# Order of ScalarE's casts at an expert's start, and a new order of all steps, in an attention and mixture-of-experts kernel

## The chip, the cores and the metric

The kernel runs on one core of a Trainium2 chip. The metric is the device time of one execution in microseconds; the median of several runs counts. TensorE (PE; PEld is its weight load) multiplies, VectorE (DVE) and ScalarE (ACT) work element by element, GpSimd (POOL) does some of that and issues the indirect DMAs, and SyncE (SP) issues all other DMAs from one queue.

## The reference

Two parts. Attention over q, k, v of shape 2 x 8 x 576 x 64: the sum of a pooled attention (q, k, v averaged over groups of 4 positions, 144 x 144 scores, the result repeated 4 times) and a local one (positions less than 4 apart). Then a mixture of 8 experts on the 1152 rows of 512:

```python
x = out.transpose(0, 2, 1, 3).reshape(B * S, H * D)        # 1152 x 512
logits = x @ w_gate                                        # 8 experts
e = argmax(logits); g = softmax(logits)[e]                 # one expert a row, up to capacity 288
y = maximum(x_e @ w1[e], 0) @ w2[e]                        # 512 -> 1024 -> 512
out[row] = g * y
```

## The kernel before

The rows are cut into ten tiles L0 to L9 (each two blocks of 58 positions), the pooled attention into eight parts P0 to P7. Routing goes in groups of tiles (K0: tiles 0 and 1, K1: 2 to 5, K3: 6 and 7, K4: 8 and 9). The experts are ranked by their number of rows and run one after the other, expert 0 first, with 192, 184, 160, 160, 152, 120, 112 and 88 row slots.

All five engines run an order that is written out by hand, in two lists of steps, `PLAN` (attention and routing, to the start of the first expert) and `PLAN2` (experts). `run` and `run2` take one step after the other and emit its instructions; each engine executes its own in this order and waits for data by semaphore. So the lists are the queues. The steps that matter here:

- `Lt.sc, mx, sb, ex, tu, ct, v0, v1, a, r, n`: scores (PE), largest and shift (DVE), exp (ACT), transpose (PE), its copy (ACT), values (PE) and their division (DVE) of tile t. `Lt.sp` spreads pooled rows by DMA, `Lt.ad` adds them (POOL; for tile 9 VectorE in two halves, `L9.ad0`, `L9.ad1`, L558), `Lt.xw` stores the rows to DRAM (SP, L584), `ga, cx, lq, lc, lg` are the gate's logits, `hi, lw` split the rows in two parts (ACT, DVE L581).
- `Pj.s, m, g, w, t, c, va, na, nr, nm`: the same for the pooled attention. `S...` and `V...` pool q, k and v, `D...` load (`Ds00` the gate's weights, `Ds10` the capacity `cap_i`, which `C` reads).
- `Kj.e0` to `e4`, `rk`, `pl`: best expert (DVE, L642 on) and rank of each row. `B.` and `R.` rank the experts. `K4.x, K4.y` give the slots' rows (PE L741, DVE L747).
- `Z`, `ZS`: one warm matmul on zeros (L176), to keep TensorE busy; ten more run at the start.
- `G`: gather of an expert's rows (POOL). `T0cp, T0c6` to `T0c9`: expert 0's rows transposed and selected into `pX` (PE, L887 to L896), where c is one of two halves; `T00h, T01h`: their cast to fp32r on ScalarE (L900), `T00l, T01l`: the remainder on VectorE (L902).
- `F`n: load of chunk n, 1 MB of weights (SP, L310); four chunks an expert, two of `w1` and two of `w2`, into five buffers. `Wia`: cast of half a chunk to fp32r (ACT, L327), `Wid`: its remainder in bf16 (DVE, some on POOL, L337). Chunk n is W2n and W2n+1: chunk 0 is W0, W1, chunk 1 W2, W3 (both expert 0's `w1`), chunk 2 W4, W5 and chunk 3 W6, W7 (its `w2`).
- `Uefp, h, f, r, l`: quarter f of expert e's first product (PE, L837 fp32r "hi", L840 bf16 "lo"), its copy, sum, Relu, remainder; its PSUM tile comes from three buffers. `D...` the second product, `Ee.p, y, s` the way out (the scatter is POOL, L989).

A fp32 product is made of three: hi x hi and hi x the remainder of the rows in one fp32r matmul of 2n columns, and the weights' remainder times the rows in bf16. A product that is not in `HI_FIRST` does the lo part first; it needs only `T..h`, the hi part also `T..l`.

```python
nc.scalar.copy(hi, r)                                              # L327, Wia
eng.tensor_tensor(lo, r, hi.bitcast(F32), op=ALU.subtract)         # L337, Wid
nc.scalar.copy(hi, self.pX[c2][:, :, 0:n])                         # L900, T0ch
```

Of the kernel before, what the change touches and what calls it, by code (L numbers as in the profile page):

```python
# [1284 lines left out]
```

## Time and profile before

| what | value |
|---|---|
| median of 3 runs | 217.24 us (216.4 to 217.84) |
| the profiled execution | 218.41 us, span 216.6 us |
| TensorE busy | 202.4 us (93%) |
| VectorE busy | 176.9 us (82%) |
| ScalarE busy | 141.1 us (65%) |
| POOL busy | 94.6 us (44%) |
| DMA | 53.55 MB, mean 247 GB/s |

The span runs from the first to the last instruction on an engine. Shares are means over stages with different limits: the attention to about 88 us, where chains run from engine to engine, and the experts after it. The chain of waits follows the end of the span back to what released each step. A number in brackets behind an instruction is the time that its engine sat idle before it, and what ended that.

### The profile page before, as it was taken

What the parts mean: (1) busy time and instruction counts of PE and PEld (TensorE: products, weight loads), DVE (VectorE), ACT (ScalarE), POOL (GpSimd) and SP (SyncE); (2) the same over time, 40 slices, a digit from 0 to 9 for tenths busy, and PEclk for the clock granted to TensorE, in tenths of its full rate; (3) what the DMA queues carried; (4) which work ended last, traced back from release to release, by engine and by line L of the source; (5) the groups of instructions that cost most, each with busy time, mean ns of one, the idle gap of its engine ahead of it and who ended that gap; (6) DMA issues with size and microseconds to landing.
All of it is one profiled execution on the core that took longest, in us unless ns stands there. A gap on an engine that the chain in (4) does not pass through costs nothing.

```text
span 216.6 us, 5906 instructions
## 1 busy us (share of the span) xinstructions
PE 202.4 (93%) x2270; PEld 175.8 (81%) x2270; DVE 176.9 (82%) x415; ACT 141.1 (65%) x289; POOL 94.6 (44%) x116
## 2 busy tenths in 40 slices
PE   8887999999979999699999999999899999999990
PEld 2565878788867779599999999999799998788880
DVE  1896879777898898589999999977999986799920
ACT  2125474567458552668668899679878989869520
POOL 6705962286241754363319238043380380533041
PEclk9999999999999999889999999999999999999997
DMA  5999977866697749958697978999989999846011
GB/s 122 360 263 211 267 255 124 252 140 179 106 343 213 192 155 289 422 183 280 228 319 297 342 295 266 310 359 357 287 335 348 346 340 326 295 135 254 2 58 34
DMA packets 16011, 53.55 MB, mean 247 GB/s; under 512 B 2059, under 2 KB 7179, under 8 KB 11880
## 3 DMA queue, kind: packets, MB, share of 16 engines
q1 hardware_dynamic: 14312, 48.51, 70.0%
q0 software_dynamic: 1664, 4.60, 6.2%
q8 instruction: 19, 0.31, 0.5%
q14 instruction: 16, 0.13, 0.2%
HBM read 45.84 MB, written 5.01 MB: 235 GB/s over the span
## 4 chain that ended last, share of the span: by engine, by line
PE 50%; DVE 21%; DMA 10%; ACT 8%; issue 6%; POOL 1%; SPq 1%; POOLq 0%; DVEq 0%; ACTq 0%
PE pH L837 10%; DVE wlo L337 8%; DMA wraw<-in_w 7%; PE pY L837 7%; PE pZ L954 5%; PE pH L840 5%; PE pY L840 3%; PE psO L518 3%; ACT whi L327 3%; PE psS L484 3%; DMA QT<-in_qT 2%; PE psG L392 2%; PE psOg L431 2%; PE psT L505 2%; PE psTg L417 2%
## 5 line engine op out<-in xcount | busy, mean ns | idle before, releaser
L337 DVE TENSOR_TENSOR wlo<-wraw,whi 128x1024 bf16<-128x1024 f32 x57 | 71.2, 1274 | 1.5 <-ACT whi L327 1.3
L327 ACT CAST whi<-wraw 128x1024 fp32r<-128x1024 f32 x64 | 64.7, 1049 | 8.1 <-DMA wraw<-in_w 7.1
L837 PE MATMUL pH<-xs,whi 128*128 128x320 f32 (+6 forms) x256 | 42.9, 313 | 0.8 <-DVE yT L971 0.7
L837 PEld LDWEIGHTS pH<-xs,whi 128*128 128x128 f32 x256 | 37.4, 193 | 1.7 <-PE pH L837 0.9
L840 PEld LDWEIGHTS <-wlo 128*128 128x128 bf16 x416 | 29.1, 97 | 6.0 <-issue 2.5
L337 POOL TENSOR_TENSOR wlo<-wraw,whi 128x1024 bf16<-128x1024 f32 x7 | 19.1, 2722 | 33.6 <-ACT whi L327 31.5
L837 PE MATMUL pY<-hs,whi 128*128 128x320 f32 (+3 forms) x160 | 29.3, 326 | 0.0
L989 POOL DMA_INDIRECT out<-y,si x13 | 16.0, 1231 | 30.4 <-ACT y L984 10.6
L868 POOL DMA_INDIRECT XG<-x_dram,gi x13 | 18.0, 1387 | 15.7 <-PE pX L891 11.1
L837 PEld LDWEIGHTS pY<-hs,whi 128*128 128x128 f32 x160 | 24.6, 188 | 0.0
L840 PE MATMUL pH<-xs,wlo 128*128 128x160 bf16 (+6 forms) x256 | 22.2, 231 | 1.8 <-ACT xs L900 1.8
L923 DVE TENSOR_TENSOR hf<-pH,hl 128x320 f32<-128x320 f32 (+6 forms) x32 | 14.3, 453 | 6.0 <-ACT hl L920 5.8
L176 PE MATMUL psW<-idle 128*128 128x512 bf16 x50 | 17.5, 429 | 1.3 <-DVE idle L171 1.0
L920 ACT COPY hl<-pH 128x320 f32<-128x320 f32 (+6 forms) x32 | 12.4, 401 | 9.2 <-PE pH L840 4.7
L925 ACT ACTIVATE hs<-hf 128x320 fp32r<-128x320 f32 (+6 forms) x32 | 13.9, 448 | 6.5 <-DVE hf L923 3.5
L558 POOL TENSOR_TENSOR x<-x,UP 128x512 f32<-128x512 f32 x9 | 11.4, 1276 | 14.8 <-DMA UP<-od 6.1
L927 DVE SCALAR_TENSOR_TENSOR hs<-hf,hs 128x320 fp32r<-128x320 f32 (+6 forms) x32 | 14.5, 471 | 2.1 <-ACT hs L925 2.0
L500 ACT ACTIVATE pt<-pt 128x512 f32<-128x512 f32 x10 | 6.3, 632 | 15.1 <-DVE pt L496 15.1
L374 POOL TENSOR_TENSOR wraw<-wraw 72x512 f32<-72x512 f32 x8 | 10.3, 1286 | 11.0 <-DMA wraw<-in_vp 11.0
L840 PE MATMUL pY<-hs,wlo 128*128 128x160 bf16 (+3 forms) x160 | 14.8, 238 | 0.0
L518 PE MATMUL psO<-VW,pT 64*64 64x65 f32 x320 | 12.3, 221 | 0.9 <-ACT pT L509 0.7
L518 PEld LDWEIGHTS psO<-VW,pT 64*64 64x64 f32 x320 | 10.5, 134 | 3.1 <-ACT pT L509 1.1
(223 smaller groups left out, 358.2 us busy)
## 6 DMA issues: line engine op xcount, KB each, us to landing
wraw<-in_w SPq DMA_DIRECT2D x32, 1024.0 KB, 7.1
x_dram<-x SPq DMA_DIRECT2D x10, 256.0 KB, 2.1
wraw<-in_vp SPq DMA_DIRECT2D x4, 576.0 KB
UP<-od SPq DMA_DIRECT2D x16, 120.0 KB, 3.4
VW<-in_vw SPq DMA_DIRECT2D x2, 780.0 KB
VW<-in_vw SPq DMA_DIRECT2D x2, 520.0 KB
QT<-in_qT SPq DMA_DIRECT2D x2, 476.0 KB
KT<-in_kT SPq DMA_DIRECT2D x2, 476.0 KB, 7.3
```

The costliest lines, as they stand in the source:

```text
L176: nc.tensor.matmul(psW, idle, idle.unsqueeze(1).to_broadcast([128, 4, 128]), start=True, stop=True)
L327: nc.scalar.copy(hi, r)
L337: eng.tensor_tensor(lo, r, hi.bitcast(F32), op=ALU.subtract)
L518: nc.tensor.matmul(psO[64 * blk:64 * blk + 64, k * (D + 1):(k + 1) * (D + 1)], self.pT[64 * blk:64 * blk + 64, hp, 64 * par:64 * par + 64] ...
L837: nc.tensor.matmul(ps[:, 0:2 * n], hi, xs[:, 0:2 * n], start=first and a, stop=last and not a, skip_group_check=True)
L840: nc.tensor.matmul(ps[:, 0:n], lo, upper_half(xs[:, 0:n]), start=first and a, stop=last and not a, skip_group_check=True)
L868: nc.gpsimd.indirect_dma_start(out=xg[0:self.ps[j], :], out_offset=None, in_=x_dram[0:rows, :], in_offset=bass.IndirectOffsetOnAxis(ap=sel ...
L920: nc.scalar.copy(hl[:, :, 0:n], self.pH[f2][:, :, n:2 * n])
L923: nc.vector.tensor_tensor(hf[:, :, 0:n], self.pH[f2][:, :, 0:n], self.hl[f2][:, :, 0:n], op=ALU.add)
L925: nc.scalar.activation(hi, hf[:, :, 0:n], AF.Relu)
L927: nc.vector.scalar_tensor_tensor(self.hs[:, f, n:2 * n], hf[:, :, 0:n], 0.0, hi.bitcast(F32), op0=ALU.max, op1=ALU.subtract)
L989: d = nc.gpsimd.indirect_dma_start(out=out[:, :], out_offset=bass.IndirectOffsetOnAxis(ap=self.token(j), axis=0), in_=self.y[j][0:p, :], i ...
```

## The change

The two lists hold the same steps in another order. Two lines of code move with it, because the exponentials of a group may now come in another order: the sum tile `rz1` is made at whichever comes first. The beginning and the end of `PLAN` and the first lines of `PLAN2` are shown, with the part of `PLAN` that concerns tiles 6 to 9; the rest of the lists is reordered in the same way. `HI_FIRST` stays.

```diff
 PLAN = """
-ZS S00q0 L0.sc ZS ZS ZS L0.mx ZS L0.sb L0.ex Dq01 Dv00 ZS Z L1.sc S00q1 L0.tu S00k0 Dp00 V000 S00k1 L1.mx L1.sb
-L1.ex L3.sc S01k0 Z S01k1 L3.mx L3.sb V001 L2.sc L1.tu L1.ct L1.v0 L2.mx L2.sb Z Ds00 L2.ex P0.s0 P0.m0 P0.m1
...
-P2.nr Dp11 P2.nm L0.cx P5.s0 L1.ad L4.a0 L4.r0 L4.n0 P5.m0 P5.m1 P5.g0 P5.w0 P3.va L1.ga V110 P5.w1 L0.lq Ds10
...
-P7.c0 L6.a1 L6.r0 P6.t1 P6.c1 L8.sc Bg C L4.ad L6.n0 P7.t1 L7.mx L8.mx L8.sb P7.c1 L6.r1 L8.ex L2.lg L6.n1 L3.lg
-K0.s1 L4.ga L4.cx L6.sp K0.s0 Bl L5.ad L5.ga P6.va P6.na L5.cx L4.xw L7.sb L6.ad P6.nr P6.nm P7.va P7.na P7.nr
-L7.ex L5.lq K0.tz K0.ts P7.nm L4.lq ZS L5.lc L7.tu L4.lc L6.hi L4.lg L5.lg L7.ct F0 K1.e0 K1.e1 K1.e2 L8.tu
-K1.z0 L7.v0 L7.v1 K1.e3 ZS L6.lw ZS K1.e4 L7.a0 K1.rk W0a W1a L6.ga ZS L7.r0 ZS F1 K1.z3 L8.ct ZS L7.a1 L7.sp
...
-K1.s3 L8.ad W2a L7.ga L9.sp K1.sl K1.to Ia W0d L9.v0 L9.v1 L9.a0 L8.ga ZS L7.cx L9.a1 ZS L7.hi L7.lw L7.lq ZS
-L6.lg L8.hi L7.lc ZS L9.r0 L9.r1 L9.n0 L9.n1 Z L6.xw L7.lg L9.ad0 K3.e0 K3.e1 K3.e2 L8.cx L9.ad1 G01 L8.lg L8.xw
-K3.e3 K3.e4 L9.ga0 ZS L8.lw K3.z0 L9.ga1 L9.xw F2 K3.z1 L9.hi L7.xw K3.rk ZS ZS L9.cx0 G00 K3.h0 K3.p0 F3 K3.q0
-ZS L9.lw L9.cx1 K3.pl L9.lg0 L9.lg1 T00p K3.tz K4.e0 K4.e1 K4.z0 K4.z1 K4.e2 K4.e3 K4.e4 Rk K4.rk K4.h0 W3a
-K4.pl K4.p0 W4a T01p K3.tn K4.tz W5a Rb Ra T016 K4.q1 K4.q0 K4.ts T006 K4.s0 Z K4.tn K3.q1 T007 F4 T017 T018
-T008 K3.s1 T009 Rc K4.s1 K3.ts T019 K3.s0 K4.x1 K4.x0 W3d K4.y1 K4.y0 ZS Rd ZS
+ZS ZS ZS Z Ds00 L0.sc L0.mx Z ZS Z L0.sb L0.ex L1.sc Dq01 ZS Z S00q0 S00k0 Z L0.tu L3.sc Dp00 S00k1 L1.mx L1.sb
+V000 L1.ex S01k0 S01k1 L2.sc Z Dv00 Dp01 S00q1 L1.tu L1.ct L3.mx L3.sb L2.mx L2.sb P0.s0 L2.ex L3.ex Z L2.tu
...
+P6.m1 P6.g0 L6.tu L6.ct P6.w0 L4.sp L5.a1 L5.r1 L5.n1 P5.va K0.e4 P5.na Ds10 P6.w1 P5.nr L2.ad P4.va P4.na P4.nr
+P4.nm P6.t0 P6.c0 P6.t1 P6.c1 K0.z0 P5.nm P7.s0 Dv11 Bk L3.ad L4.ad P7.m0 P7.m1 L3.ga L3.cx P7.g0 Bb L2.ga L6.v0
+L6.v1 C L2.cx P7.w0 L2.lq L2.xw L5.sp L5.ad L3.lq L6.a0 L6.sp L7.sc Bc Bd Be Bf Bh Bg Bl L6.a1 K0.rk L6.r0 L3.lc
+L2.lc K0.z1 L6.r1 P7.w1 L6.n0 F0 P7.t0 P7.t1 P7.c0 L8.sc L7.mx L7.sb L7.ex L8.mx P7.c1 L2.lg K0.pl L4.ga L4.cx
+L3.xw P6.va L6.n1 P6.na P6.nr L8.sb L5.ga K0.tz L6.ad P7.va P7.na L5.cx L4.xw L5.lq L5.lc L4.lq L3.lg P6.nm
+P7.nr K0.s1 P7.nm L1.xw L6.hi L4.lc ZS L5.xw L7.tu L5.lg L8.ex L7.ct L4.lg L7.sp L8.tu L7.v0 L6.lw K1.e0 K1.z1
...
+ZS Ia L7.hi L8.ad L9.v0 L9.v1 L9.sp G01 L9.a0 L7.ga W0d L9.a1 ZS L9.r0 L9.r1 ZS L8.ga L9.n0 L7.xw ZS L9.n1 L6.xw
+L7.cx L8.hi L7.lq L9.ad0 L6.lg L9.ad1 ZS L8.cx L7.lw L7.lc L7.lg K3.e0 K3.e1 G00 L8.xw L8.lw L9.xw L9.ga0 ZS
+K3.e2 K3.e3 ZS L9.hi L9.lw L9.cx0 L8.lg K3.z0 K3.e4 K3.z1 L9.ga1 L9.cx1 K3.h0 Z Z K3.rk K3.p0 F1 F2 K3.pl K3.tn
+L9.lg0 L9.lg1 K4.e0 K4.e1 K4.z0 K4.z1 K3.q0 K3.tz K4.e2 K4.e3 T00p F3 K4.e4 K4.h0 K4.rk K4.p0 K3.q1 F4 Rk K4.pl
+Rb K4.s0 K4.s1 Ra T01p T016 Z T017 K3.ts K3.s0 K4.q0 K4.tz T018 Rc K4.ts K4.tn ZS K4.q1 K3.s1 W2a W3a W2d T006
+T007 T008 T009 T019 K4.x0 K4.x1 W3d ZS K4.y1 ZS ZS K4.y0
...
 PLAN2 = """
-T00h T01h T00l W6a T01l Re W7a Ib W5d W6d U01p U01h U00p W8a W2d U03p U00h F5 W9a U01f G10 U00f U02p U00r Is
-U00l U03h U01r U03f U01l U03r W4d U03l G11 U02h U02f F6 Rf Rg G21 F7 W10a D010 Rl W11a U02r D000 W7d T11p U02l
...
-W61a W62a W58d W54d D60p E40s U63l U62l U71h U70h W59d D61p W60d U70f W63a U71f W63d U70r W61d U71r U72p U72h
-E60y E50s E41y E41s U73p U70l U73h U71l U72f W62d U72r U72l E60s U73f U73r U73l D70p D71p E70y E70s
+T00h T01h W4a W5a W6a F5 F6 T00l T01l W7a U01p U01h U00p Rd Re Ib Rf Is W6d G10 U00h U00f U02p U03p U01f Rg W8a
+U00r U00l U02h W4d W5d U01r U01l U03h D000 G11 U02f G21 W9a D010 U02r Ic W10a G20 U02l U03f T10p W7d F7 Rl F8
...
+W60a W59d D60p U72p W60d U70f U63r U63l D61p U73p W61a W62a U71h U71f W61d W63a U70r W62d E41s U71r U72h U70l
+U72f U71l D70p E40p U73h U73f E60y U72r U73r E60s W63d E40y E40s U73l U72l D71p E70y E70s
...
@@ -624,7 +624,7 @@
-            self.used = 0
+            self.used, self.z = 0, None
...
         def total(self, i):
-            if i == 0:
+            if self.z is None:
                 self.z = self.small("rz1")
```

## Rows read from the trace of the kernel before

**Rows 1.** Chain of waits, 79 to 98 us: start, duration in us, what.
```profile
79.61 8.38 DMA wraw<-in_w
...
88.96 1.04 ACT whi L327
...
90.43 1.50 PE pH L840 x8
91.93 3.76 PE pH L837 x16
95.69 0.70 PE pH L840 x8
96.39 1.42 PE pH L837 x8
```

**Rows 2.** Stretches of one us: PE, PEld, DVE, ACT, POOL busy, PEclk, DMA share, GB/s.
```profile
89.00:90.00 1.00, 0.00 (x0) 0.00 (x0) 0.00 (x0) 1.00 (x3) 0.00 (x0) 1.00 0.97 410
...
91.00:92.00 1.00, 1.00 (x7) 0.94 (x6) 1.00 (x2) 0.91 (x1) 1.00 (x1) 0.50 1.07 451
```

**Rows 3.** Timeline, 78 to 93 us: start, busy, instruction [idle before <- its releaser].
```profile
78.64 0.42 DVE L558 TENSOR_TENSOR x<-x,UP 128x256 f32<-128x256 f32 x1
...
80.42 0.68 DVE L581 TENSOR_TENSOR xpb<-x,xpb 128x512 fp32r<-128x512 f32 x1
...
81.31 0.17 DVE L642 TENSOR_REDUCE rmn<-psl 128x2 f32<-128x16 f32 x1
...
86.75 1.06 PE L896 MATMUL pX<-pick,xpb 128*128 128x192 f32 x8
...
87.65 0.56 PE L741 MATMUL psI<-tg,sel 128*128 128x24 bf16 x16
88.01 1.99 ACT L327 CAST whi<-wraw 128x1024 fp32r<-128x1024 f32 x2 [4.67 <-DMA wraw<-in_w]
...
88.05 0.43 DVE L747 TENSOR_TENSOR sums<-psI,sums 128x48 f32<-128x48 f32 x2 [0.79 <-PE psI L741]
...
89.91 0.85 ACT L900 CAST xs<-pX 128x384 fp32r<-128x384 f32 x2
...
90.41 1.02 DVE L902 TENSOR_TENSOR xs<-pX,xs 128x384 fp32r<-128x384 f32 x2 [1.81 <-ACT xs L900]
...
91.09 1.99 ACT L327 CAST whi<-wraw 128x1024 fp32r<-128x1024 f32 x2 [0.33 <-DMA wraw<-in_w]
```

**Rows 4.** TensorE's expert stage as one stretch: PE busy, PEclk, DMA share, GB/s.
```profile
90.40:205.30 114.90, 113.94 (x966) 0.99 0.80 285
```

**Rows 5.** Weight tile wraw: its remainders (ns min/median/max), its loads' landing.
```profile
L337 DVE TENSOR_TENSOR wlo<-wraw,whi x57: 1204/1215/2647, 68.3 to 205.0; 128x1024 bf16<-128x1024 f32 x57
...
DMA to landing us min/median/max: 5.1/7.1/8.4
```

**Rows 6.** Timeline, VectorE at the first step of group K1.
```profile
65.57 0.19 DVE L642 TENSOR_REDUCE room<-psl 128x4 f32<-128x32 f32 x1 [0.64 <-PE psl L615]
```

**Rows 7.** Chain of waits, warm matmuls between 33 and 54 us.
```profile
35.87 0.22 PE psW L176
...
42.01 0.32 PE psW L176
...
47.07 0.32 PE psW L176
```

**Rows 8.** Timeline, first warms and the first pooled maxima.
```profile
1.05 4.56 PE L176 MATMUL psW<-idle 128*128 128x512 bf16 x11 [1.05 <-DVE idle L171]
...
17.51 0.82 DVE L401 TENSOR_REDUCE mxg<-psG 72x2 f32<-72x288 f32 x2 [0.88 <-PE psG L392]
```

**Rows 9.** The page's DMA issue of cap_i; spreads and Bb in the timeline.
```profile
cap_i<-in_cap SPq DMA_DIRECT2D x1, 1.0 KB, 7.9
...
38.37 9.80 SPq L552 DMA_DIRECT2D UP<-od  x7
...
53.66 0.15 DVE L772 SCALAR_TENSOR_TENSOR keyB<-psC,rev 128x8 f32<-128x8 f32 x1
```

More of the change, by code (lines that the diff above doesn't have):

```diff
@@ new lines @@
+V001 V010 V011 S01q1 L4.mx L4.sb L2.ct P0.t0 L0.a0 ZS P0.c0 L0.r0 P0.t1 L0.a1 L0.r1 L0.n0 L0.n1 P1.s0 P1.m0
+P1.m1 P0.c1 L2.v0 P0.va L3.tu P1.g0 P1.w0 Z ZS P1.w1 P1.t0 L2.a0 L2.r0 L2.n0 P0.na P0.nr L3.ct P2.s0 Z P1.t1
+P1.c0 Z L4.ex P0.nm P1.c1 Dq10 L2.v1 P2.m0 P2.m1 P2.g0 P2.w0 P1.va V100 L2.a1 Dq11 L2.r1 S10q0 P2.w1 P3.s0 Dv01
+P1.na P2.t0 P2.c0 P1.nr P1.nm V101 P3.m0 L4.tu P3.m1 P3.g0 P3.w0 P3.w1 P2.t1 S10k0 L4.ct S10k1 S10q1 L6.sc S11k0
+P3.t0 L0.sp L1.sp P3.c0 L2.n1 L6.mx L5.sc L6.sb L0.ad P2.c1 S11k1 L5.mx L4.v0 P3.t1 L1.ad P3.c1 L5.sb L5.ex Dp11
@@ new lines @@
+Dv10 P2.va P2.na P5.s0 P2.nr L0.ga L4.a0 L4.r0 P2.nm P3.va V110 L0.cx L1.ga L4.n0 P5.m0 P5.m1 L0.lq P3.na P5.g0
+P5.w0 P3.nr P3.nm L2.sp P5.w1 L1.cx L4.v1 S11q0 S11q1 P4.s0 L1.lq L4.a1 L4.r1 P4.m0 L0.lc L0.lg L1.lc P4.m1
+P4.g0 P5.t0 P4.w0 L4.n1 P4.w1 L5.tu L5.ct L1.lg K0.e0 L3.v0 L3.a0 K0.e1 K0.e2 L3.v1 L3.r0 L3.a1 L3.n0 P6.s0
+L3.r1 L3.n1 L3.sp P5.c0 V111 P4.t0 P6.m0 P4.c0 P5.t1 L5.v0 L5.a0 P5.c1 L5.r0 L5.n0 L6.ex L5.v1 K0.e3 P4.t1 P4.c1
+P6.m1 P6.g0 L6.tu L6.ct P6.w0 L4.sp L5.a1 L5.r1 L5.n1 P5.va K0.e4 P5.na Ds10 P6.w1 P5.nr L2.ad P4.va P4.na P4.nr
@@ L109 @@
-U52h U52f U51r W47d U52r E31p U60p E30s U51l F28 U53h E31y T70h W51d U53f T71p W50d T70l F29 D41h F30 U60h D41t
-U61p T71h U53r U53l D50p W54a U52l D51p U61h U61f U60f T71l W55a W56a W57a W56d U60r U61r U63p W58a E40p W57d
-U60l U63h U62p E31s U61l W52d E20s E40y U62h U70p E50y U63f W59a W53d W60a U62f E41p U62r U63r W55d U71p F31
-W61a W62a W58d W54d D60p E40s U63l U62l U71h U70h W59d D61p W60d U70f W63a U71f W63d U70r W61d U71r U72p U72h
-E60y E50s E41y E41s U73p U70l U73h U71l U72f W62d U72r U72l E60s U73f U73r U73l D70p D71p E70y E70s
+T00h T01h W4a W5a W6a F5 F6 T00l T01l W7a U01p U01h U00p Rd Re Ib Rf Is W6d G10 U00h U00f U02p U03p U01f Rg W8a
@@ new lines @@
+U00r U00l U02h W4d W5d U01r U01l U03h D000 G11 U02f G21 W9a D010 U02r Ic W10a G20 U02l U03f T10p W7d F7 Rl F8
+U03r W11a U03l W12a T10h T11p T11h D011 W13a D001 W10d W8d G31 W9d T11l T10l W14a T20p T21p W15a D00h W14d D00t
+W13d U11p W11d T20h T21h T20l D01h D01t W16a W17a G30 F9 U11h U10p G40 U10h T21l U11f E00p E00y U10f W12d W18a
+W19a W15d U12p U13p W16d U10r F10 F11 T31p E01p W17d U21p U11r U11l W18d U13h U10l E01y U12h U13f T30p T30h U20p
+U12f U13r E00s G41 F12 W19d Id U12r U13l U21h W20a U21f W21a W22a U12l W23a D100 U20h W20d F13 D101 W21d D10h
@@ new lines @@
+D10t D110 T31h W24a W25a W26a D111 T31l W27a D11h U22p T30l U20f F14 T41p W25d E01s U20r U22h G70 W24d W26d U21r
+U23p U20l U21l W28a F15 U22f U22r T40p W23d U23h D11t W22d D200 U23f W29a T40h T41h U30p U23r W29d U23l U22l
+D201 W28d W27d F16 U31p U30h W30a T41l W31a W32a F17 U30f W31d E11p D20h D210 G50 T40l W32d W33a W34a D20t U31h
+E11y W33d W35a U31f F18 D211 U30r U30l D21h D21t E11s U31r U31l U32p W36a U32h W34d U32f W37a F19 F20 W35d W38a
+U33p W30d D310 U33h W39a T50p T50h T50l F21 U33f E21p U32r U40p E21y W40a U40h D300 T51p U33r W41a U32l U33l
@@ new lines @@
+E10p D301 T51h W36d U40f W42a D30h W43a W38d W39d U41p W37d D30t G60 T51l U41h F22 W44a D311 E21s F23 F24 W41d
+U42p U41f U40r T60p U41r W40d U43p W43d D31h E10y U40l D31t U42h U43h W42d U43f W45a U50p E30p U41l F25 F26 U51p
+T60h U42f T60l D400 U42r U42l W45d E10s U50h E20p U43r U43l U50f W46a W47a W48a W47d E20y W49a D401 D40h U51h
+E30y W44d D410 W50a D40t D411 W51a T61p U51f D41h W49d E30s E31p W48d T61h D41t U52p T61l W52a U50r W46d U51r
+U51l F27 U52h U52f U50l E31y U52r W53a W54a E31s U61p F28 F29 W51d U61h U52l W55a T70p U53p W50d D50p W54d U53h
```

33 lines of the change are left out of this document (6 added, 27 removed).

## The prediction

> **What bounds the kernel now.** I read the chain of waits in order of time first, then the one-microsecond stretches around the place where it leaves the engines, then the engines' timeline there, then the waits. The reader should see this in the chain [rows 1]: the second half of the last row tile of the attention is added at 78.64 us on VectorE and done at 79.06 [rows 3]; behind it the SP queue issues a 1 MB weight load at 79.61, which takes 8.38 us; ScalarE casts that chunk; then it casts the first expert's gathered rows (89.91 [rows 3]); then TensorE's products start (90.43). The loads are the casts' only reason to wait: the two casts at 88.01 sat 4.67 us before them [rows 3]. They are W4a and W5a, halves of chunk 2, the first half of expert 0's second matrix, which nobody needs before its first `down`. T00h and T01h stand behind them on ScalarE, although TensorE had the transposed rows ready at 86.75 + 1.06 = 87.81. So TensorE stands still: 0.00 us busy in 89 to 90 [rows 2]. [...]
>
> From there to the end TensorE is the bound: 113.94 of 114.90 us busy between 90.40 and 205.30 [rows 4]. So the first hi product's start (91.6) sets the end, and a shift of it is a shift of the end, as long as the expert stage stays that dense.
>
> **The change part by part.** Both step lists hold the same 986 steps, 40 warm matmuls among them. No operation is added or removed; the edit of `total` only creates the sum tile at whichever exponential is emitted first. So all is order.
>
> *Hand-over, the loads.* Before, F0 and F1 (chunks 0, 1) are issued early and F2 waits behind L9.xw. After, only F0 is early; F1 is moved on SP past L7.sp, L3.xw, L8.sp, L1.xw, L5.xw, L9.sp, L6.xw, L8.xw and L9.xw, and F1, F2, F3, F4, F5 follow L9.xw in a row. Those stores and spreads are issued one load's slot (about 0.5 us) earlier; they feed POOL and the gathers, not this chain, and I cost that at nothing. F1 therefore starts where F2 did, 79.61 - 79.06 = 0.55 us after the second L9.ad1. That step comes earlier: L7.lw (0.68, as the row of its neighbour) and K3.e0 to e2 (3 x 0.17, as the row of K4.e0) no longer stand before it [rows 3], so it ends at 79.06 - 1.19 = 77.87 and F1 goes at 78.42. K4.e0 stays at 81.31, since the same VectorE steps stand before it in another order; so do the routing and the last pX at 87.81.
>
> *Hand-over, the casts.* ScalarE's order becomes W2a W3a T00h T01h W4a to W7a U01h. The wait for chunk 2 goes, a wait for chunk 1 takes its place. Landing of F1: not below 5.1 us, the shortest of 32 loads, and the nearest row is the 8.38 of F2 at the same place; the median is 7.1 [rows 5]. I take 7.7, between the median and the neighbour: 86.1. W2a and W3a take 1.99 [rows 3] to 88.1, T00h and T01h 0.85 more. On VectorE, W2d and W3d (1.215 each [rows 5]) now stand before T00l: W2d starts at 87.15, W3d ends at 89.6, K4.y1 and K4.y0 (0.43) at 90.0, T00l and T01l (1.02 [rows 3]) at 91.05. The first hi product reads these lo halves: 91.05 against 91.6, a gain of 0.5. In short, the hi products start 4.95 after chunk 1 lands, and no sooner than pX allows: K4.x ends at 88.21, then 0.43 + 1.02 gives 89.7. Bounds: gain 1.9 (landing in 5.1) to loss 0.1 (8.38).
>
> The stand changes shape: TensorE has three warms instead of two after K4.x (0.4 each, to 89.1), then 0.7 of lo products, then stands 1.3 us instead of 1.8 [rows 2]. [...]
>
> W4a to W7a now stand before U01h. Queued behind: U01h, U00h and with them the buffer for U03p. W6a waits for F3, two chunk spacings behind F1 (91.09 - 88.01 = 3.1 us each [rows 3]: 92.3); W7a ends at 94.3, U01h, U00h, U00f and U01f follow at about half a microsecond each, as T00h and T00l, to 96.3. U03p wants the buffer after U01p's hi products and two more quarters: 91.05 + 1.42 + 2 x (0.70 + 1.42) = 96.7 [rows 1]. This is covered by 0.4; if F3 lands later than that cover, U03p stands for the excess.
>
> *Attention, routing wait.* VectorE sat 0.64 us before K1.e0, waiting for the logits psl [rows 6]. The logits' ScalarE copies stood behind L7.ex, which stood behind L7.sb, itself behind two selections. After, L7.sb comes right after L7.mx and the copies come earlier, and L6.lw is done ahead of K1.e0. From there VectorE is dense to the last tile, so I take -0.6; bounds 0 and -0.64.
>
> *Attention, warms.* Five warms between P3.s0 and L7.sc become none; three of them lie on the chain, 0.22, 0.32 and 0.32 long [rows 7]. Bounds -0.86 and 0 (another wait takes their place); I take -0.4. The warms moved to the end stand in waits that are there anyway.
>
> *Start.* Four warms instead of one precede L0.sc: eleven warms took 4.56 us [rows 8], so three cost 1.2, and the first pooling add now stands behind L0.sb instead of filling that time. VectorE idles 0.88 us at 17.5 for scores [rows 8], where the lag can be made up. Loss 0.4, bounds 0 and 1.2. Ds10 (cap_i) goes behind L4.sp and its reader C comes earlier. Its landing took 7.9 us for 1 KB; issued when the seven spreads to L4.sp are out, at 48.2, it lands by 56.1 at worst, and C, right behind Bb (to 53.8), would hold VectorE for 2.3 us [rows 9]. Before, it was issued right behind the load Dp11; after, only spreads are ahead of it, so I cost it at nothing.
>
> *Experts and tail.* The same products; the stage has 0.96 us of idle [rows 4], the most that a new order can win by filling gaps. A new gap would cost about the same. I take 0, bounds -1 and +1. In the tail E40p and E40s move between E60s and E70s; TensorE runs D71p in the meantime, so they are covered; without that cover one more scatter is about 1 us.
>
> **Sum.** -0.5 - 0.85 - 0.6 - 0.4 + 0.4 = -1.95 us. Against the profiled execution (218.41, its span 216.6 and 1.8 around it) this gives 216.4; the median of the runs is 217.24, 1.2 below it, so 215.2.
>
> **The rivals.**
> [...]
> *One wait for another.* F1 takes 8.38 as F2 did: hi products at 91.75, the clock falls as before. Only the attention's -0.6 is left: 216.6. For it: same place, same stores ahead.
> *The load lands late* (slower). Five loads in a row instead of four share the engines. If F1 lands one chunk spacing (3.1 us) later than F2 did, after 11.5 us, the hi products start at 94.85, 3.2 later, and with -0.6 the time is 219.8. It decides from a landing of 11.0 us on. Against: no load of this trace took more than 8.4 [rows 5].
>
> **How the numbers follow.** Chances: forecast 0.38 (its own range 214.0 to 216.2), in time 0.24, one wait for another 0.23, late 0.10, attention or experts worse by 2 us or more 0.05. About 1% (2.2 us) is what a measurement of this kernel can tell from no change. Faster by over 1% (under 215.07): all of the second, somewhat under half of the forecast, 0.43. Slower (over 219.4): the late load and a part of the last, 0.13. Within 1%: 0.44. The range 212.6 to 218.2 takes in the second case with its spread and the third with an attention that wins nothing.
>
> **What would show it.** In the changed kernel's timeline: T00h directly behind W3a, and the wait before W2a ended by a load; F1's landing; hi products 4.95 us after it; K1.e0 without idle before it; TensorE's stand before U01p's hi products under 1.5 us, and the clock in the stretch behind it. I am wrong if the last pX moves by more than 1.5 us either way (the attention's order then matters more than the hand-over), if F1 lands outside 6.5 to 8.4 us, or if TensorE's idle in the expert stage differs from 1 us by more than 1.

## The result

The changed kernel takes 219.84 us (median of 4 runs, 219.37 to 219.97), the kernel before beside it 216.86 (216.40 to 217.84): 1.0128 times as long, 95% interval 1.0086 to 1.0170. It is slower, where 215.2 was forecast. The profiled execution took 219.97 us, its span 218.3. All ratios here compare the runs of each kernel that lie within 1.5% of its fastest, and since the kernel before spreads by more than that, medians of all runs stand beside them below.

The chain of waits of the changed kernel, start, duration in us, what:

```profile
73.75 1.97 POOL XG L868
...
76.03 6.92 DMA XG<-x_dram,gi
...
82.99 2.08 PE pX L889 x8
...
86.03 1.71 PE pX L889 x8
...
92.00 0.42 PE psI L741 x16
...
92.77 0.93 DVE xs L902 x2
```

Before, the chain ran through a weight load there [rows 1]. Now it runs through the gather of the first expert's rows (G00, step of GpSimd, line 868), and through its transposes (T00p, line 889). The timeline of the same kernel, 76 to 100 us, a number in brackets being the idle time before the instruction and what ended it:

```profile
76.84 2.68 SPq L310 DMA_DIRECT2D wraw<-in_w  x5
...
82.70 1.99 ACT L327 CAST whi<-wraw 128x1024 fp32r<-128x1024 f32 x2 [1.27 <-DMA wraw<-in_w]
...
82.99 2.08 PE L889 MATMUL pX<-ident,XG 128*128 128x128 f32 x8 [2.47 <-DMA XG<-x_dram,gi]
...
85.35 0.17 DVE L721 SCALAR_TENSOR_TENSOR rpr<-psR,rme 128x16 f32<-128x16 f32 x1 [3.79 <-PE psR L696]
...
91.59 0.93 ACT L900 CAST xs<-pX 128x384 fp32r<-128x384 f32 x2 [6.89 <-PE pX L896]
```

The five loads F1 to F5 go out at 76.84, 0.8 us after the second gather's issue. Chunk 1 is there in good time: its cast starts at 82.70, 5.9 us after the issue. But the gather lands 6.9 us after its issue. Before, T00p started without a stand at 81.28, so the gather took at most 3.6 us from its issue at 77.66:

```profile
77.66 1.05 POOL L868 DMA_INDIRECT XG<-x_dram,gi  x1 [0.31 <-issue]
...
81.28 1.16 PE L889 MATMUL pX<-ident,XG 128*128 128x128 f32 x8
```

In the changed kernel TensorE stands 2.47 us, and behind T00p in its queue stand the counts of K4, for which VectorE waits 3.79. One-microsecond stretches of the changed kernel (columns as in [rows 2]):

```profile
75.00:76.00 1.00, 1.00 (x14) 0.48 (x12) 1.00 (x4) 1.00 (x3) 0.72 (x1) 1.00 0.06 12
...
79.00:80.00 1.00, 0.95 (x15) 0.95 (x14) 0.50 (x4) 0.00 (x0) 0.10 (x2) 1.00 1.03 360
...
82.00:83.00 1.00, 0.01 (x1) 0.01 (x1) 0.00 (x0) 0.30 (x1) 0.71 (x2) 0.50 1.04 434
...
87.00:88.00 1.00, 1.00 (x7) 1.00 (x7) 0.90 (x8) 0.00 (x0) 0.00 (x0) 0.50 1.06 451
88.00:89.00 1.00, 1.00 (x9) 0.96 (x9) 1.00 (x4) 0.00 (x0) 0.00 (x0) 0.90 0.97 410
```

The DMA engines do nearly nothing while the gather is being issued (12 and 9 GB/s from 75 to 77), and are full from 79 us on (360 to 451 GB/s), with the weight loads just issued, when its data should move. After the stand the granted clock is at 0.50 to 88: T00p's eight matmuls take 2.08 us, 1.16 before. The last pX ends at 92.00, 87.81 before [rows 3].

So three stretches make the difference. Second gather's issue: 77.66 before, 76.03 after, -1.63: the attention is faster in this pair. From there to the first hi product (line 837): 13.97 before, 17.49 after, +3.52. From there to the end: 124.97 and 124.78, -0.19. Sum +1.70, which is 218.3 - 216.6. The middle one splits: from the gather's issue to T00p it takes 6.96 instead of 3.62 (+3.34, so T00p starts 1.71 later), from T00p to the end of pX 9.01 instead of 6.53 (+2.48), and from there to the hi products 1.52 instead of 3.82 (-2.30). That -2.30 isn't yet the price of moving the casts, for with pX this late the loads have had more time too; e1 below moves the casts alone.

### The profile page after: what moved, and what is told of

It reads as the page before. It is cut to its first block, busy times and chain, and to the rows that moved or that the text cites. A ratio compares the mean times of both kernels' runs of the same rounds, so it can differ in the third digit from the quotient of the medians.

```text
span 218.3 us, 5907 instructions
## 1 busy us (share of the span) xinstructions
PE 201.8 (92%) x2270; PEld 177.0 (81%) x2270; DVE 179.5 (82%) x415; ACT 141.7 (65%) x289; POOL 98.1 (45%) x116
## 4 chain that ended last, share of the span: by engine, by line
PE 62%; DVE 23%; issue 5%; DMA 3%; POOL 2%; ACT 2%; POOLq 0%; DVEq 0%; ACTq 0%
PE pH L837 13%; PE pY L837 9%; PE pH L840 6%; DVE wlo L337 5%; PE pZ L954 5%; PE psW L176 4%; PE pY L840 4%; DMA XG<-x_dram,gi 3%; PE psO L518 3%; PE psOg L431 3%; PE pZ L979 2%; DVE mx L492 2%; DVE pt L496 2%; PE pX L896 2%; PE pX L889 2%
## 5 line engine op out<-in xcount | busy, mean ns | idle before, releaser
L337 DVE TENSOR_TENSOR wlo<-wraw,whi 128x1024 bf16<-128x1024 f32 x57 | 74.2, 1329 | 0.9 <-ACT whi L327 0.9
L837 PE MATMUL pH<-xs,whi 128*128 128x320 f32 (+6 forms) x256 | 41.8, 308 | 1.1 <-DVE hf L923 1.1
L837 PEld LDWEIGHTS pH<-xs,whi 128*128 128x128 f32 x256 | 36.7, 189 | 1.8 <-DVE hf L923 1.4
L989 POOL DMA_INDIRECT out<-y,si x13 | 17.8, 1366 | 33.0 <-ACT y L984 17.3
L337 POOL TENSOR_TENSOR wlo<-wraw,whi 128x1024 bf16<-128x1024 f32 x7 | 18.6, 2657 | 25.3 <-ACT whi L327 19.9
L868 POOL DMA_INDIRECT XG<-x_dram,gi x13 | 19.8, 1525 | 21.4 <-DVE sf L1057 12.6
L840 PE MATMUL pH<-xs,wlo 128*128 128x160 bf16 (+6 forms) x256 | 21.5, 228 | 0.0
L558 POOL TENSOR_TENSOR x<-x,UP 128x512 f32<-128x512 f32 x9 | 11.4, 1271 | 13.9 <-DMA UP<-od 12.4
L927 DVE SCALAR_TENSOR_TENSOR hs<-hf,hs 128x320 fp32r<-128x320 f32 (+6 forms) x32 | 15.7, 497 | 0.9 <-ACT hs L925 0.7
L374 POOL TENSOR_TENSOR wraw<-wraw 72x512 f32<-72x512 f32 x8 | 10.5, 1317 | 10.4 <-DMA wraw<-in_vp 10.4
L518 PEld LDWEIGHTS psO<-VW,pT 64*64 64x64 f32 x320 | 10.4, 134 | 2.5 <-issue 1.2
```

The costliest lines, as they stand in the source:

```text
L518: nc.tensor.matmul(psO[64 * blk:64 * blk + 64, k * (D + 1):(k + 1) * (D + 1)], self.pT[64 * blk:64 * blk + 64, hp, 64 * par:64 * par + 64] ...
L837: nc.tensor.matmul(ps[:, 0:2 * n], hi, xs[:, 0:2 * n], start=first and a, stop=last and not a, skip_group_check=True)
L840: nc.tensor.matmul(ps[:, 0:n], lo, upper_half(xs[:, 0:n]), start=first and a, stop=last and not a, skip_group_check=True)
L868: nc.gpsimd.indirect_dma_start(out=xg[0:self.ps[j], :], out_offset=None, in_=x_dram[0:rows, :], in_offset=bass.IndirectOffsetOnAxis(ap=sel ...
L927: nc.vector.scalar_tensor_tensor(self.hs[:, f, n:2 * n], hf[:, :, 0:n], 0.0, hi.bitcast(F32), op0=ALU.max, op1=ALU.subtract)
L989: d = nc.gpsimd.indirect_dma_start(out=out[:, :], out_offset=bass.IndirectOffsetOnAxis(ap=self.token(j), axis=0), in_=self.y[j][0:p, :], i ...
```

## Experiments

The stretches of each kernel's profiled execution, in us, cut as above, and its time against the kernel before:

| kernel | second gather issued | gather to hi products | hi products to end | span | median (of before beside it) | ratio to before, 95% |
|---|---|---|---|---|---|---|
| before | 77.66 | 13.97 | 124.97 | 216.6 | | |
| changed | 76.03 | 17.49 | 124.78 | 218.3 | 219.84 (216.86) | 1.0128 (1.0086 to 1.0170) |
| e1_casts_only | 78.67 | 11.57 | 126.06 | 216.3 | 217.91 (214.30) | 1.0116 (1.0039 to 1.0194) |
| e2_loads_held | 76.03 | 21.88 | 122.89 | 220.8 | 223.09 (214.30) | 1.0461 (1.0377 to 1.0544) |
| e3_early_and_held | 76.91 | 12.73 | 125.36 | 215.0 | 218.99 (214.30) | 1.0268 (1.0187 to 1.0348) |
| e4_rank_before_gather | 77.37 | 16.98 | 124.85 | 219.2 | 220.42 (214.30) | 1.0241 (1.0177 to 1.0305) |
| e5_loads_first | 79.18 | 16.90 | 123.22 | 219.3 | 220.93 (216.83) | 1.0248 (1.0124 to 1.0372) |
| e6_cheap_hold | 80.52 | 14.07 | 125.21 | 219.8 | 217.17 (216.83) | 1.0076 (1.0020 to 1.0132) |
| e7_early_cheap_hold | 77.26 | 17.05 | 125.09 | 219.4 | 220.09 (216.83) | 1.0207 (1.0084 to 1.0330) |
| a0_after_again | 74.66 | 18.04 | 125.10 | 217.8 | 219.57 (216.83) | 1.0184 (1.0062 to 1.0305) |
| e9_no_pool | 74.64 | 16.31 | 124.05 | 215.0 | 217.38 (216.78) | 1.0105 (1.0019 to 1.0191) |
| e8_hold_and_no_pool | 75.77 | 13.97 | 124.66 | 214.4 | 216.84 (216.78) | 1.0033 (0.9986 to 1.0081) |
| e10_casts_no_pool | 76.97 | 11.46 | 125.07 | 213.5 | 217.65 (216.78) | 1.0021 (0.9952 to 1.0091) |
| e11_before_no_pool | 76.80 | 13.04 | 126.66 | 216.5 | 217.75 (216.78) | 1.0037 (0.9945 to 1.0128) |
| e13_f1_early_hold | 79.39 | 12.21 | 125.00 | 216.6 | 217.49 (216.79) | 1.0140 (1.0048 to 1.0233) |
| e12_f1_early_hold_no_pool | 78.46 | 12.21 | 124.13 | 214.8 | 216.31 (216.79) | 1.0068 (1.0007 to 1.0129) |
| b0_before_again | 77.61 | 12.60 | 122.59 | 212.8 | 216.34 (216.79) | 0.9990 (0.9903 to 1.0076) |
| e14_f1_in_gap | 78.72 | 12.71 | 124.67 | 216.1 | 216.66 (216.37) | 1.0160 (1.0082 to 1.0237) |

All three stretches wander between executions of one kernel: the kernel before gave 77.66, 13.97 and 124.97 and then (b0) 77.61, 12.60 and 122.59; the changed kernel 76.03, 17.49 and 124.78 and then (a0) 74.66, 18.04 and 125.10. The first column wanders most, in part because in some executions TensorE's clock was at 0.50 for some us in the attention: 63 to 69 us in e1, 64 to 70 in e5, 20 to 26 in e6, 21 to 23 in e14. One stretch of e1:

```profile
64.00:65.00 1.00, 1.00 (x6) 1.00 (x7) 0.33 (x2) 0.56 (x1) 0.00 (x0) 0.50 0.53 205
```

So the lines of each timeline carry the verdicts, and differences of a stretch only where they are larger than this. Medians and ratios compare a kernel with the kernel before run beside it on the same chip.

**Taken apart: the casts alone, and the loads held.**

```diff
 e1 (before):  -W4a -W5a in the first list; T00h T01h +W4a +W5a T00l
 e2 (changed): -F1 F2 K3.pl        +K3.pl H F1 F2
 e3 (changed): F0 +F1 ... L9.sp +F2 ... -F1 F2 K3.pl  +K3.pl H
 H: nc.sync.dma_start(out=gt_dram[0], in_=pos[:, 6:7])   # 128 x 4 bytes
 e4 (changed): on TensorE, T00p behind K4.rk and Rk
```

H is a small store into scratch that waits for K3.pl, so that what stands behind it on the SP queue waits too: in e8 below, with H of 4 bytes, H goes out at 79.86 and the first load at 80.36, where it went at 76.84 in the changed kernel.

> The kernel before, with one part of the change alone: W4a and W5a stand behind T00h and T01h on ScalarE. Theory (the new cast order is good, what lost time is the gather that the row of loads delays): T00h starts at about 87.9 us instead of 89.9, the first hi products of expert 0 at 89.7 to 90.0 instead of 91.6, TensorE stands under 1 us, the granted clock stays at 1.00; the time is 213 to 215 us, some 2 to 3.6 under the kernel before. Rival (the cast order itself loses, because U01h and so the PSUM buffer of U03p wait behind the casts): no gain, 217 us or more, and TensorE waits at U03p or later.

> The changed kernel, with one small store on the SP queue ahead of F1 that waits for K3.pl on VectorE (its content is read by nobody), so that the five loads start at about 80.2 us instead of 76.8 and the gather has the DMA engines alone. Theory (loads issued right behind the gather delay it): the gather of expert 0 lands within 4.5 us of its issue at 76, T00p does not wait for it, the clock does not fall at 82; F1 lands near 86, hi products start near 91; 217 us, 2 to 3 under the changed kernel. Rival (the gather is late for a reason of its own: its descriptors on POOL, its rows' stores): T00p still starts at 83.0, the loads come later on top, 220 us or more.

> As the kernel with the held loads, but F1 right behind F0 and F2 behind L9.sp, so that only F3 to F5 are held by the small store. Theory: the gather lands by 80.5, the casts W2a and W3a are done long before T00h, the last pX ends near 87, hi products start at 88.5 to 89, the clock stays at 1.00: 213 to 214 us, under both kernels. Rival (the new attention order or the cast order lose by themselves): 217 us or more with the hi products at 91 or later.

> The changed kernel, with T00p behind K4.rk and Rk on TensorE, so that the routing of the last two tiles is not queued behind the wait for the gather. The gather stays late. Theory (3.8 us of VectorE's wait for psR come from the queue order on TensorE behind T00p, and are part of the loss): VectorE's wait for K4.rk is gone, the last pX ends 1 to 2 us earlier (90 to 91 instead of 92.0), 218 to 219 us. Rival (only the gather's landing and the clock count, the picks are not what the selection waits for): last pX at 92 as before, 219.8 us.

e1: the hand-over works by itself: gather to hi products 11.57 instead of 13.97 (12.60 in b0), with the clock at 1.00 there. Yet it isn't faster but 3.6 us longer than the kernel before beside it: it is 1 us longer behind the hi products (below), and its profiled execution lost the clock in the attention. The 213 to 215 expected was missed. e2: the gather is in time, T00p starts at 80.35 without a wait; that part of the theory holds. The clock is at 0.50 from 81 to 84 all the same, with TensorE busy, and no run here shows why. The time got worse for another reason, the store itself. One stretch of e2, and ScalarE in its timeline:

```profile
85.00:86.00 1.00, 1.00 (x11) 0.99 (x9) 0.41 (x2) 0.00 (x0) 0.00 (x0) 1.00 1.32 49
```

```profile
93.00 1.99 ACT L327 CAST whi<-wraw 128x1024 fp32r<-128x1024 f32 x2 [11.58 <-DMA wraw<-in_w]
```

Behind a store of 0.5 KB in 128 pieces the DMA engines move 49 GB/s in that stretch, and the 1 MB load behind it lands 12.3 us after its issue. e3, with two loads ahead of the gather, has T00p in time (0.24 us of wait) and the hi products at 89.64; F3 behind the small store came late (a cast waits 2.83), and its median missed the expected 213 to 214 by 5 us. e4 was a miss: with T00p behind K4's counts TensorE's queue is free, but the gather still lands 7.2 us after its issue and T00p waits 0.89, clock at 0.50. From T00p to the end of pX it takes 8.26 us, 0.75 less than in the changed kernel, so K4's late counts were the smaller part of the 2.48. What has to change is the transfer, not who waits for it.

**Is it the loads? In the kernel before, and with a store that costs nothing.**

```diff
 e5 (before):  L9.ga1 +F2 F3 F4 L9.xw ; later F2 F3 F4 removed
 e6 (changed): as e2, H with out=gt_dram[0][0:1], in_=pos[0:1, 6:7]   # 4 bytes
 e7 (changed): as e3, H of 4 bytes
 a0: the changed kernel once more
```

> The kernel before, with its loads F2, F3 and F4 issued before the store L9.xw instead of behind it and later ones: three 1 MB loads in a row right at the gather's time, as the changed kernel has five. Nothing else moves. Theory (loads delay the gather): the gather G00 (issued at about 77.7 us) lands 5 us or more after its issue instead of 3.6, T00p stands 1.5 us or more before its matmuls, the last pX comes at 89.5 or later (87.81 in the kernel before), and the time is level or up to 1% longer, since the load of chunk 2 and so T00h come earlier and pay part of it back. Rival (the gather was late for its own reasons, the order of stores and spreads ahead of it): it lands within 4 us of its issue, the last pX stays within 0.5 us of 87.8 and the time falls by 0.5 us or more.

> The changed kernel with F1 to F5 held on the SP queue behind a store of 4 bytes that waits for K3.pl (about 80 us). It is the earlier run with the held loads again, with one piece of 4 bytes in place of 128. Theory (two causes: loads delay the gather, and the 128 pieces jammed the queue): the gather lands in time (T00p stands under 0.5 us), F1 lands 5 to 6 us after its issue at about 80.5, so 86, W2a and W3a follow pX without a wait over 1 us, T00h by 88.8, hi products by 91.0, 2.5 us earlier than in the changed kernel, time 2 us or more under it. Rival (loads after 80 us are slow whatever stands ahead of them): F1 takes 8 us or more again, W2a waits over 4 us, the time is at or over that of the changed kernel.

> The changed kernel with F1 right behind F0 (as in the kernel before), F2 behind L9.sp, and F3 to F5 held behind the store of 4 bytes. Theory: nothing moves on the DMA engines while the gather does, and chunks 1 and 2 are there in time: last pX at 88 or before, T00h directly behind it, hi products by 90.0 (1.6 us before the kernel before), W6a waits under 1 us for F3; the stands at about 96 and 116 stay (1 us each), so the time is 1 us under the kernel before to level with it. Rival (the expert order costs nothing): those stands shrink with F3 in time and the time is 2.5 us or more under the kernel before.

> The changed kernel itself once more, beside the others on the same chip, so that each has both kernels as its measure. Theory (the loads delay the gather, by order and not by chance): gather landing 6 us or more after its issue, T00p stands about 2.5 us, hi products 93 to 94, ratio to the kernel before 1.008 to 1.02. Rival (one execution's bad luck): the gather lands within 4.5 us in this execution and the ratio is under 1.005.

e5's timeline shows the fault put into the kernel before:

```profile
76.72 2.61 SPq L310 DMA_DIRECT2D wraw<-in_w  x3
...
79.18 1.04 POOL L868 DMA_INDIRECT XG<-x_dram,gi  x1 [0.31 <-issue]
...
86.39 2.07 PE L889 MATMUL pX<-ident,XG 128*128 128x128 f32 x8 [3.46 <-DMA XG<-x_dram,gi]
```

Three loads ahead of the gather's data: landing 7.2 us after the issue, T00p stands 3.46. Only the place of F2 to F4 was changed (the stores L9.xw and L7.xw, which the gather, already issued, doesn't wait for, come behind them). e6 takes it out of the changed kernel: T00p without a wait, gather to hi products 14.07 instead of 18.04, its median 217.17 beside 219.57 for the changed kernel on the same chip: -2.4. (e6's profiled execution took 221.63 where ten others took 216.0 to 218.6; only the stretch around the gather is read from it.) e7 fell: T00p stands 2.07, because F2, issued at 72.41 just ahead of the last rows' stores, moved at 79 to 81 beside the gather, where the DMA engines carry 383 to 400 GB/s. The changed kernel repeats itself closely, 219.27 to 219.63, T00p standing 2.53. Over all 18 profiles it took 5.5 to 7.2 us from the gather's issue to T00p in e7 and in the five where the row of loads went out between 2.5 us ahead of it and 0.8 us behind it, and 3.6 to 4.5 in the twelve others.

**The experts: GpSimd's remainders.** VectorE's remainder of a weight half takes 1.22 us, in the changed kernel once 4.05. The tile's row and the timeline of the changed kernel:

```profile
L337 DVE TENSOR_TENSOR wlo<-wraw,whi x57: 1207/1216/4054, 67.4 to 207.2; 128x1024 bf16<-128x1024 f32 x57
```

```profile
95.87 4.05 DVE L337 TENSOR_TENSOR wlo<-wraw,whi 128x1024 bf16<-128x1024 f32 x1
96.43 2.41 POOL L337 TENSOR_TENSOR wlo<-wraw,whi 128x1024 bf16<-128x1024 f32 x1
100.44 1.65 PE L837 MATMUL pH<-xs,whi 128*128 128x384 f32 x8 [1.09 <-DVE hf L923]
...
113.40 4.57 DVE L337 TENSOR_TENSOR wlo<-wraw,whi 128x1024 bf16<-128x1024 f32 x2
114.32 2.57 POOL L337 TENSOR_TENSOR wlo<-wraw,whi 128x1024 bf16<-128x1024 f32 x1
118.42 0.90 PE L979 MATMUL pZ<-ident,yT 128*128 128x128 f32 x4 [1.39 <-DVE xs L902]
```

Both times a remainder on GpSimd (W5d, W15d) meets one on VectorE: W5d begins 0.56 us into it, W15d at 114.32, 0.2 us before the second of the two in that row (114.53, 3.43 us by itself). VectorE ends about 1.1 us after GpSimd does, and TensorE stands behind it: 1.09 + 1.39 = 2.48 us. Before, W5d ran at 90.08 and met no remainder on VectorE; W15d met one that took 2.31 us, with no stand of TensorE behind it. With the casts alone (e1) W15d meets one for longer, and TensorE stands:

```profile
112.32 4.07 DVE L337 TENSOR_TENSOR wlo<-wraw,whi 128x1024 bf16<-128x1024 f32 x1
112.89 2.41 POOL L337 TENSOR_TENSOR wlo<-wraw,whi 128x1024 bf16<-128x1024 f32 x1
116.85 0.41 PE L979 MATMUL pZ<-ident,yT 128*64 128x128 f32 x2 [1.22 <-DVE xs L902]
```

So W5d and W15d were put on VectorE, in their places:

```diff
-WP = (5, 15, 23, 31, 39, 47, 55)
+WP = (23, 31, 39, 47, 55)
```

e9 does that to the changed kernel, e8 to e6, e10 to e1, e11 to the kernel before.

> The changed kernel with the first two of the seven remainders that GpSimd computes (W5d and W15d) on VectorE, in their places. Theory (GpSimd's remainder holds VectorE's for its whole length: 4.05 and 3.4 us where 1.22 is normal, and TensorE stands 1.09 at 100 and 1.39 at 118 behind it): VectorE's remainders between 94 and 117 take 1.22 each, both stands fall under 0.3 us, the time falls by 1.5 to 2.5 us, although VectorE has 2.4 us more to do. The gather stays late. Rival (VectorE is simply full there, 29.8 of 30 us busy): the extra 2.4 us make the stands longer, the time is level or longer.

> Both remedies on the changed kernel: F1 to F5 held behind a store of 4 bytes until K3.pl, and W5d and W15d on VectorE. Theory (two separate losses that add up): the hold gives 2.4 us as measured before, the remainders 1.5 to 2.5 us more: 4 to 5 us under the changed kernel, 1 to 2 us under the kernel before. Rival (the two losses hide each other): no more than 0.7 us under the kernel with the hold alone.

> The kernel before with W4a and W5a moved behind T00h and T01h, as in the earlier run with the casts alone, and with W5d and W15d on VectorE. Theory: the hand-over's gain (hi products at 90.2 instead of 91.6, clock not halved) stays and the stands at 96 (0.63) and 117 (1.22 and 0.45) go, so 2 us or more under the run with the casts alone, and 0.5 to 2.5 us under the kernel before. Rival (the stand at 117 is not the collision but the order of the casts): stands of over 1 us remain in 95 to 118 and the time stays over that of the kernel before.

> Control: the kernel before with W5d and W15d on VectorE and nothing else. There GpSimd's W5d ran while VectorE was idle (90.08 to 92.46) and W15d beside a remainder that cost 0.9 us with no stand of TensorE behind it. Theory: nothing to win, within 0.7 us of the kernel before, or a little longer. Rival (two remainders less on GpSimd help any order): 1 us or more under the kernel before.

The timeline of e9:

```profile
97.07 2.35 DVE L337 TENSOR_TENSOR wlo<-wraw,whi 128x1024 bf16<-128x1024 f32 x2
...
99.95 0.96 PE L837 MATMUL pY<-hs,whi 128*128 128x384 f32 x4 [0.35 <-DVE hs L927]
```

These two collisions are gone, and so are the two stands; the mechanism is shown. Its size was half missed: hi products to end falls from 125.10 to 124.05, 1.05 us, and not 1.5 to 2.5, while VectorE has 2.4 us more to do and TensorE stands 0.35, 0.67 and 0.69 at other places. The rest of the 2.8 us between the spans of a0 and e9 lies ahead of the hi products, where the edit changes nothing: in e9 the gather landed 5.5 us after its issue and T00p stood 0.96. e9's median is 217.38 (10 runs) against 219.57 for the changed kernel on another chip; that comparison holds no better than their two ratios, whose intervals overlap. e8 is 216.84 beside e6's 217.17, again on other chips; that the two remedies add up as expected is not shown. e10 has hi products at 88.43 and no stand over 0.82 from 63 us on, yet its runs spread from 215.0 to 221.3 and its median is 0.9 us over that of the kernel before, where 0.5 to 2.5 under it was expected. Its stretch behind the hi products is still 2.5 us longer than b0's; two later remainders on GpSimd meet VectorE's there (3.02 and 3.31 us, at 124.58 and 140.87), and what the rest is stays open. e11: nothing to win, as expected.

**Why the kernel before spreads.** Its times lie between 210.7 and 221.1 us over all runs here, those of the changed kernel between 219.3 and 220.0.

```diff
 e13 (changed): F0 +F1 ; -F1 F2 K3.pl  +K3.pl H F2          (H of 4 bytes)
 e12: e13 with W5d and W15d on VectorE
 e14: e8 with F1 moved ahead of L9.xw:  L8.xw +F1 L8.lw L9.xw
 b0: the kernel before once more
```

> The changed kernel with F1 right behind F0, and F2 to F5 held behind the store of 4 bytes. It is the earlier run with F1 and F2 early, with F2 put back into the held row: one step differs. Theory (there F2, issued half a microsecond ahead of the last rows' stores, ran beside the gather): with F2 held the gather lands in time (T00p stands under 0.4 us), last pX 7 us or less after T00p's start, hi products 9 to 10 us after it, and the time is 2 us or more under that run's 220.1. Rival (an early F1 delays the attention's own transfers or the hold is at fault): T00p stands 1.5 us or more again, time at 219 or over.

> The same with W5d and W15d on VectorE: all three remedies on the changed kernel, the version that should beat both. Theory: gather in time, chunk 1 there before pX ends, so TensorE stands under 0.7 us between pX and the lo products (1.31 with F1 held), full clock from there, no stand over 1 us in the expert stage: 214 to 215.5, 1 to 2 us under the kernel with all loads held, and its times within 1.5 us of each other. Rival (F1's place is worth nothing): within 0.5 us of that kernel's 216.8.

> The kernel before, profiled beside them. Its times spread from 213.3 to 220.3, the changed kernel's from 219.3 to 220.0. Theory (the same collision by chance: F2 goes right behind the last rows' store, and whether the gather has landed by then differs from one execution to the next): time falls as the granted clock rises, and the profile of a fast one (under 215.5) shows T00p without a wait, chunk 2 there earlier and a stand before the lo products under 1 us, of a slow one (over 218) T00p or the casts waiting 2 us or more. Rival (it is the expert stage): hi products start within 0.5 us of 15 us after the second gather's issue (77.66 to 91.63 in the first profile: 14.0), and the difference lies behind them.

> The changed kernel with W5d and W15d on VectorE, F2 to F5 held behind the store of 4 bytes, and F1 alone ahead of the last store L9.xw, at about 73 us, where the DMA engines are nearly idle for 3 us and no transfer of the attention is left in line. Theory (a load costs what stands behind it in line at that moment): the gather is no later than with all loads held (T00p without a wait over 0.3 us), no wait of the attention for a store, chunk 1 lands by 80, the casts W2a and W3a come before pX ends, TensorE stands under 0.8 us before the lo products (1.31 with F1 held), hi products 9.7 us or less after T00p's start, 1 us or more under the kernel with all loads held (216.8): 214.5 to 216, and 0.3 to 1 percent under the kernel before. Rival (any load within 3 us of the gather delays it): T00p stands 1 us or more, time at 217.5 or over.

The chain of b0, and a stretch of it, against [rows 1, 2]:

```profile
79.56 7.37 DMA wraw<-in_w
...
89.76 0.68 PE pH L840 x6
90.44 2.80 PE pH L837 x16
```

```profile
91.00:92.00 1.00, 1.00 (x7) 1.00 (x7) 0.93 (x4) 1.00 (x2) 0.43 (x1) 1.00 1.01 426
```

The same kernel; the load of chunk 2 lands 1.0 us sooner (7.37 instead of 8.38), TensorE stands 0.82 instead of 1.77, the clock stays full, sixteen matmuls take 2.80 instead of 3.76, and the span is 3.8 us shorter. So the theory (the gather, by chance) fell in part: between these two executions the hand-over differs, but by the load of chunk 2, not by the gather. Of the 3.8 us, 1.42 lie before the hi products, 1.04 between there and the next transposes (104.68 against 102.22), and 1.35 behind 119 us, which I didn't follow.

Two executions don't explain the spread, and other runs speak against the hand-over as its only source. In e10 the cast T00h waits for no load, and its runs spread as widely. In e11, whose clock is at 1.00 from the attention to the last expert, a load comes late deep in the experts, and TensorE stands 2.88 us:

```profile
153.80 1.05 ACT L327 CAST whi<-wraw 128x1024 fp32r<-128x1024 f32 x1 [3.42 <-DMA wraw<-in_w]
...
157.36 0.63 PE L979 MATMUL pZ<-ident,yT 128*128 128x128 f32 x4 [2.88 <-DVE xs L902]
```

Over 101 recorded runs of the kernel before, the time goes with the mean granted clock: 38 runs at 0.994 or more have a median of 214.6 us, 27 at 0.985 or less one of 218.5. The profiles show the clock falling at different places, and what starts a fall isn't taken apart: in e8 TensorE stands 1.31 us ahead of its lo products and the clock stays at 1.00, in e9 it stands 0.96 ahead of T00p and the clock is at 0.50 behind it.

e13 settles e7: with F2 held T00p doesn't wait, gather to hi products 12.21 instead of 17.05. But its attention is later, for VectorE now waits for a store that stands in line behind F1:

```profile
69.33 0.42 DVE L535 TENSOR_TENSOR x<-psO,rz 128x256 f32<-128x256 f32 x1 [1.31 <-DMA x_dram<-x]
```

From the first counts of K1 to the second gather's issue it takes 12.4 us (67.01 to 79.39), 10.4 in the changed kernel. So it is in all profiles: 11.8 to 12.5 in the four runs with F1 behind F0 (e3, e7, e12, e13), 10.4 in every run of the changed order without it. Of the rival, the delay of the attention's own transfers is there; its stand of T00p and its time of 219 are not. e14 puts F1 where nothing waits in line: from the same counts 10.4 us again (68.31 to 78.72), T00p without a wait, no stand for any load. Its rival fell too: F1, issued 2.6 us ahead of the second gather, didn't make it late. But its profiled execution began late: TensorE waits 1.52 us for the keys at 13.71, the clock is at 0.50 from 21 to 23 behind that, and the step of line 478 that has waited 0.61 us for pg comes at 35.14, in the changed kernel at 32.38. Its median is 216.66 (12 runs, 214.1 to 217.9), over the 214.5 to 216 expected, beside 216.37 for the kernel before. e12, all remedies with F1 early, missed its 214 to 215.5: 216.31 (12 runs, 213.9 to 219.2), its stands from 90 us on 0.35, 0.67 and 0.69, what it gained behind the gather spent ahead of it (12.1 us from the counts of K1). No version here is shown to beat the kernel before. e8 shows what is left: its mean granted clock is 0.986 or more in all ten runs, and they take 216.2 to 217.5 us, where the kernel before beside it took 214.6 in the median of its twelve runs with a clock of 0.994 or more. So with both remedies the changed order still loses about 2 us to the kernel before at its best. Against b0 its profile is 1.8 us earlier at the second gather and loses 1.4 and 2.1 us in the two stretches behind it; the 2.1 weren't followed.

## Why the prediction was wrong

**The attention** was right in sign, and too small if one goes by the pair of profiles: the forecast had the last addition end at 77.87 and F1 go at 78.42; they came at 76.26 and 76.84. Where the clock was full in the attention, the second gather is issued at 76.8 to 77.7 in the old order (before, b0, e10, e11) and at 74.6 to 77.4 in the new one (changed, a0, e2, e4, e8, e9), so 1.5 us earlier in the mean, though the ranges overlap. Its terms weren't taken apart by a run. The wait at K1.e0 is gone, cap_i (3.2 us) held nothing up.

**The step that failed** is "K4.e0 stays at 81.31 ... so do the routing and the last pX at 87.81", together with "they feed POOL and the gathers, not this chain, and I cost that at nothing". K4.e0 came at 80.33, but the gather became the chain: last pX at 92.00. I followed F1 past nine stores and spreads on its own queue and asked how soon it lands; I didn't ask what five loads do to the transfer that was just under way on GpSimd's queue. Before, one load went out 1.9 us behind the gather's issue; now five go out 0.8 us behind it. Which of the two matters more, the number or the time, no run separates. The forecast weighed the loads only against each other. What the trace shows is a gather that took at most 3.6 us before and takes 6.9 beside the five loads. My own sign of error, a last pX that moves by more than 1.5 us, is what came.

**The loads and the casts.** F1 landed 5.9 us after its issue, not 7.7, so chunk 1 was there by 82.7, where the forecast took 86.1. From the last pX to the hi products it took 2.30 us less than before, where a gain of 1.9 bounded the forecast. T00h waited for pX (6.89 us), for no load. U03p did stand, 1.09 us (line 837 at 100.44), but not for F3: the casts W4a to W7a ran in a row to 96.30. What held its PSUM buffer was VectorE's sum (line 923), behind the remainder that had met GpSimd's; I had followed the queue on ScalarE only. The time of the rival "the load lands late", 219.8, is what was measured, and that is luck: no load of this hand-over was late, the gather was.

**The clock** was costed in the wrong place. The -0.85 of the sum, taken for a shorter stand before the lo products, is shown by no run. Behind that stand the kernel before had its clock at 0.50 [rows 2] and took 1.72 us longer for 24 matmuls than at the pace of the rows after them, 3.76 - 2 x 1.42 + 1.50 - 0.70 [rows 1]; the -0.85 is about half of that. For a stand as long as the one forecast, 1.3 us ahead of the lo products, e8 shows the case: 1.31 us, with the clock at 1.00 behind it, so half of the 1.72 was too little there. In the changed kernel the clock fell at the gather instead, to 0.50 from 82 to 88, and pX, with K4's late counts, took 2.48 us longer.

**The experts at nothing** came out (-0.19) by luck. Against b0, whose clock stays full, the changed kernel's stage is 2.2 us longer, about the 2.48 us that TensorE stands behind W5d and W15d; and the first profile of the kernel before is 2.4 us longer than b0's, 1.04 of it up to the next transposes, where its clock was at 0.50, the rest not followed. I had the row with 2647 ns as the longest remainder [rows 5] and didn't ask what made it twice the median.

**The base.** The sum went from an execution of 218.41 us that had itself lost the clock at the hand-over; b0 took 214.58. A part of the gain was therefore one that the kernel before has anyway in its better executions, and subtracting 1.2 for the median didn't cover that. (218.41 - 1.95 - 1.17 is 215.3, not 215.2; nothing hangs on it.)

## What to carry to other kernels

When a load is moved earlier, list every transfer that is under way or in line at its new time, on all queues, and what waits for each; here a gather that landed 3.3 us late cost more than the load's early landing gained (3.34 and 2.48 us against 2.30). Judge a new order by what its instructions now run beside: here two remainders that met on VectorE and GpSimd took back what the casts had won. Profile the kernel before more than once before summing against it: two executions of it differed by 3.8 us, 2.5 of them where one load landed 1 us sooner and the clock stayed full.
